# Attention and a SiLU feed-forward on one Trainium2 core: three products of the last eight token tiles done by seven quarter-size products each

## The chip, the cores and the metric

The kernel runs on one core of a Trainium2 chip. The metric is the time of one execution on the device, in microseconds (us). The engines are named as in the profile: PE (TensorE, matmuls), PEld (its weight loads), DVE (VectorE), ACT (ScalarE), POOL (GpSimd) and SP (SyncE, which here only issues stores).

## The reference

Eight batches of twelve heads of attention (448 tokens, head size 64), then a feed-forward with a SiLU gate over all 3584 tokens:

```python
scores = scale * np.matmul(q, k.transpose(0, 1, 3, 2))      # (8, 12, 448, 448)
attn = exp(scores - max) / sum
x = (attn @ v).transpose(0, 2, 1, 3).reshape(3584, 768)
h = x @ w_in                                                 # (3584, 2048)
g = h / (1.0 + np.exp(-h))
out = g @ w_out                                              # (3584, 768)
```

## The kernel before

One Python function plans the whole order of work. It holds a model of the engines' times and of the buffers that come free (`Op`, `Order`, `Ring`, `Banks`), goes through time event by event, lets each engine take the ready instruction with the lowest time plus bias, and at the end records all instructions in that order. So each engine's order is fixed when the program is built, and any new instruction can shift its neighbours.

**Stages.** Scores, exponentials and the product with V of the eight batches come first, with the first feed-forward layer (`ffn1`) of earlier batches between them. The last four batches do the first layer in two groups of two batches (`PAIRS`), with seven products in place of eight (`pair_product`; PE rows `f`, DVE adds of L881, ACT copies of L877 and gates of L889). The gated values lie in `G` as 128 partitions of the feed-forward dimension, 16 blocks `f`, by tokens; the seventh token tile of every second batch lies in `X`. `w_in_t` and `w_out_t` hold the weights.

**The second layer** is out = g @ w_out. Its unit is a "quad" `qd`: a pair of token tiles of 128 tokens, 14 pairs in all. Pair 0 is done by plain matmuls (`plain`). Pairs 1 to 13 each use the seven-product scheme on a 2 x 2 split: rows are the two tiles a and b, the inner dimension is cut into blocks 0 to 7 and 8 to 15, and the 768 output columns into two halves of `OH` = 384. `product(qd, m, ...)` (L678 by way of `times`) does product m: eight matmuls of 128 x 128 weights, which are gated values or sums of them, against 384 columns of `W_[m]`. `W_[1]`, `W_[2]`, `W_[3]` and `W_[7]` are parts of `w_out_t`, of which part 7 has been overwritten with a difference; `W_[4]`, `W_[5]` and `W_[6]` are sums in own tiles (names `D`). The sums of tile rows are made on DVE by `combine_g` (L911) into three tiles `S`; sum 7 overwrites `G`.

The products add up in banks of PSUM, and reads between them take the state out:

```python
BANK = {1: 1, 6: 1, 7: 1, 4: 1, 2: 2, 5: 5, 3: 5}
OUT = {1: (0, 0), 5: (1, 1), 6: (0, 1), 4: (1, 0)}   # ACT copies the bank (take_copy, L999)
SUM = {2: (0, 0), 7: (1, 1), 3: (0, 1)}              # DVE adds the bank (take_sum, L1013)
```

So bank 1 holds 1, then 1+6, then 1+6+7, then 1+6+7+4. The four parts (i, j) of the output, tile i and column half j, are gathered in SBUF tiles `ost` of 128 x 384 floats; when a part is complete `store` (L992) issues it, four issues of 32 rows on SP for most tiles, fewer and partly on ACT's queue for pairs 12 and 13. Pairs 11 and 13 (`FAR`) have their `ost` in old `xT` buffers, pair 8 (`WIDE`) in two old `E` buffers, and the others in a ring of four (`NOST`).

`queue_quad` (L1520) queues the products in the order 1, 5, 6, 2, 7, 3, 4; the last pair's order is 1, 5, 6, 7, 3, 4 and then 2 in two halves of 192 columns, whose reads and stores are `take_end` (L1005, L1009). The planner moves single matmuls among these to fill waits.

Of the kernel before, what the change touches and what calls it, by code (L numbers as in the profile page):

```python
# [9 lines left out]
FP16 = mybir.dt.float16  # L10
# [23 lines left out]
def act(n):  # L34
    return n * 0.00087 + 0.13
# [6 lines left out]
class Ring:  # L42
# [8 lines left out]
    def when(self, n):  # L51
        return heapq.nsmallest(n, self.free)[-1] if len(self.free) >= n else None
# [162 lines left out]
def kernel(  # L215
# [736 lines left out]
    def bank(qd, m):  # L952
        return pr_t[(qd, m)][:, 0:OH]
# [3 lines left out]
    def ost(qd, i, j):  # L957
        name = f"ost_{qd}_{i}{j}"
        if qd in FAR:
            t = sb.tile([128, 3, S], FP16, name=name, tag="xT", bufs=NX3)  # L960
            t = t.rearrange("p c t -> p (c t)")[:, 0 : 2 * OH].bitcast(FP32)
        elif qd == WIDE:
            at, x = int(i != j), j
            if at not in wide_t:
                wide_t[at] = sb.tile(
                    [128, HG, S], FP16, name=f"wide_{at}",
                    tag=f"E{e_slot[f'sx_{PAIRS[0]}_{at + 1}']}", bufs=1,
                )
            t = wide_t[at].rearrange("p h s -> p (h s)").bitcast(FP32)
            t = t[:, S * x : S * x + OH]  # L970
        else:
            t = sb.tile([128, OH], FP32, name=name, tag="ost", bufs=NOST)
        ost_t[(qd, i, j)] = t
        return t

    def store(qd, i, j):
        u, t = divmod(2 * qd + i, NT)
        w, turn = 0, 0
        while w < 4:
            r, col = divmod(128 * t + 32 * w, S)  # L980
            b = 2 * u + r
# [10 lines left out]
            eng.dma_start(out=dst, in_=ost_t[(qd, i, j)][32 * w : 32 * (w + n), :])  # L992
            w, turn = w + n, turn + 1
# [3 lines left out]

    def take_copy(qd, m):
        nc.scalar.copy(out=ost(qd, *OUT[m]), in_=bank(qd, BANK[m]))  # L999
        if m == 4:  # L1000
            store(qd, *OUT[m])

    def take_end(p, c0, c1):
# [3 lines left out]
        for lo, eng in ((0, nc.sync), (64, nc.scalar)) if c0 else ((0, nc.sync),):  # L1007
            hi = lo + 64 if c0 else 128
            eng.dma_start(out=out[row + lo : row + hi, c0:c1], in_=t[lo:hi])  # L1009

    def take_sum(qd, m):
        t = ost_t[(qd, *SUM[m])]
        nc.vector.tensor_tensor(out=t, in0=bank(qd, BANK[m]), in1=t, op=ALU.add)  # L1013
        store(qd, *SUM[m])


    units = []
    for b in range(B):
# [304 lines left out]

    def queue_pair_f(pb, f):
        done, lo = {}, f"w{f // 4 * 4}"
        before = chain[-1] if chain else None
        chain.append(done)

# [154 lines left out]
    def plan_sums():  # L1483

        if not quads:
            return
        qd, todo = quads[0]
        if len(todo) == 4:
            gates = {}
            for f in range(NFF):  # L1490
                gates[f] = gates_at(2 * qd, f) + gates_at(2 * qd + 1, f)
                if None in gates[f]:
                    return
            gates_of[qd] = gates
# [22 lines left out]
        if not todo:  # L1517
            quads.pop(0)

    def queue_quad(qd):  # L1520
        quads.append((qd, [5, 6, 7, 3]))
        took = {}
        home = far_ring if qd in FAR else wide_ring if qd == WIDE else ost_ring

        def read(m, deps):
            def then(at):
                if m in (2, 3, 4):
                    leave_bank(f"p_{qd}_{BANK[m]}")(at)
                if m in (2, 3, 4, 7):
                    home.give(at + STORE)  # L1530

            fn, eng = (take_copy, "ACT") if m in OUT else (take_sum, "DVE")
            busy = act(OH) if eng == "ACT" else OH / 960.0 + 0.13
            bias = -2 if eng == "ACT" else -4
            took[m] = od.add(Op(eng, busy, lambda: fn(qd, m), deps, bias, then=then))

        def queue(m, f0, f1, c0=0, c1=OH):
            first = {6: (1,), 2: (1,), 7: (6, 5), 3: (5, 6) if qd == LAST else (5, 6, 7), 4: (7,)}.get(m, ())

            def run():  # L1540
                strips = od.mode == "cols" and bool(qk_seq or av_seq)
# [22 lines left out]
                read(m, [op] + [took[x] for x in {2: (1,), 7: (5,), 3: (6,)}.get(m, ())])  # L1564

            def deps():
# [12 lines left out]
                return made + [x[0], (x[1], 4 * mm(OH))]  # L1579

            rings = ((home, 1),) if m in OUT and f0 == 0 else ()
            moe.append((deps, int(BANK[m] == m and f0 == 0), run, rings))


        begun = {}
        for m in (1, 5, 6, 2, 7, 3, 4) if qd < LAST else (1, 5, 6, 7, 3, 4):
            for f0 in range(0, HF, 1):
                queue(m, f0, f0 + 1)
        if qd == LAST:
# [350 lines left out]
    while True:  # L1940
# [2 lines left out]
        plan_pair()  # L1943
        plan_silu()
        plan_sums()
        soon = od.step()
        if od.free["PE"] <= od.now:
            ran = False
# [80 lines left out]
```

## Time and profile before

| | us |
|---|---|
| median of 3 runs (lowest to highest) | 379.64 (379.21 to 380.22) |
| the profiled execution, its own time | 379.18 |
| its span, first to last instruction | 377.4 |
| granted PE clock over the span | 0.998 |
| last stage, second layer of pairs 10 to 13: start to end | 338.4 to 373.9 |
| last matmul starts | 373.64 |
| last DVE read starts, and takes | 373.92, 0.36 |
| last store is issued (SP and ACT both) | 374.31 |

Rows of a group read: line, engine, operation, output<-input, shapes, count | busy us, mean ns of one | idle us of the engine just before them, and who ended it. Rows in order of time read: start us, length us, engine, line, operation, output<-input, shape, count, and in brackets the engine's idle time before. Rows that follow each other without a gap are merged, so two instructions that overlap in the pipe show a length below the sum of their own.

### The profile page before, as it was taken

The page shows a single profiled execution, that of the slowest core. Times are in us where ns is not written, and L with a number is a line of the kernel's source. Part 1 is how long each engine was busy: PE and PEld are TensorE (multiplying, and loading weights), DVE is VectorE, ACT ScalarE, POOL GpSimd, SP SyncE. Part 2 cuts the span into 40 slices and gives each one's busy share as a digit, 9 for nine tenths or more (in the row PEclk, how much of TensorE's full clock was granted, in tenths as well). Part 3 has the DMA queues.
Part 4 walks back from the last instruction along what each step waited for, and adds up shares of the span by engine and source line. Part 5 has one row for each costly group of instructions (what it writes and reads, how often), then busy time and mean ns, then how long its engine had stood idle before and what let it go on. Part 6 is the DMA issues. An engine that isn't in the chain of part 4 may idle for free.

```text
span 377.4 us, 9846 instructions
## 1 busy us (share of the span) xinstructions
PE 371.1 (98%) x3982; PEld 184.8 (49%) x3982; DVE 272.0 (72%) x556; ACT 255.5 (68%) x400; POOL 85.0 (23%) x155
## 2 busy tenths in 40 slices
PE   7999999999999999999999999999999999999996
PEld 3365445444444444444444444545556655556664
DVE  3668859989995969995969998898475424446441
ACT  4988873897878697868788777658872238882221
POOL 6652348333016326006423200000000000000000
PEclk9999999999999999999999999999999999999999
DMA  7999999918049849147955411200002330001332
GB/s 120 187 207 210 207 203 194 189 25 125 17 99 151 150 50 131 19 104 103 172 87 73 54 43 44 64 23 0 0 3 62 85 94 12 0 0 49 99 108 83
DMA packets 35982, 34.47 MB, mean 91 GB/s; under 512 B 11872, under 2 KB 35168, under 8 KB 35936
## 3 DMA queue, kind: packets, MB, share of 16 engines
q0 software_dynamic: 25312, 22.82, 40.8%
q1 hardware_dynamic: 10144, 10.48, 10.3%
q8 instruction: 31, 0.51, 0.5%
q10 hardware_dynamic: 480, 0.54, 0.4%
q14 instruction: 15, 0.12, 0.1%
HBM read 45.61 MB, written 11.01 MB: 150 GB/s over the span
## 4 chain that ended last, share of the span: by engine, by line
PE 95%; ACT 3%; DMA 1%; DVE 0%; issue 0%; POOLq 0%
PE p L678 32%; PE h L678 21%; PE f L678 16%; PE s L441 11%; PE a L563 8%; PE o L678 3%; ACT E L497 2%; PE a L549 2%; PE a L596 2%; DMA rk<-in_k_dram 1%; ACT T L486 1%; PE z L678 0%; PE p_2r L678 0%; DVE KT L390 0%; DVE ost L1005 0%
## 5 line engine op out<-in xcount | busy, mean ns | idle before, releaser
L497 ACT ACTIVATE E<-s 128x896 f16<-128x896 f32 x164 | 141.9, 921 | 24.5 <-PE s L441 24.5
L678 PE MATMUL h<-xT,w_in_t 128*32 128x448 f16 (+2 forms) x762 | 83.5, 348 | 0.0
L678 PEld LDWEIGHTS <-w_in_t 128*128 128x128 f16 (+1 forms) x909 | 54.6, 97 | 50.0 <-issue 8.1
L678 PEld LDWEIGHTS <-G 128*128 128x128 f16 (+1 forms) x684 | 44.0, 97 | 32.4 <-issue 5.0
L347 POOL DMA_DIRECT2D V<-in_v_dram x88 | 48.4, 561 | 50.1 <-PE a L563 29.2
L710 ACT ACTIVATE th<-h 128x448 f16<-128x448 f32 x67 | 36.6, 546 | 24.3 <-PE h L678 20.7
L678 PE MATMUL p<-w_out_t,G 128*128 128x384 f16 (+2 forms) x334 | 51.9, 324 | 0.0
L999 ACT COPY ost<-p 128x384 f32<-128x384 f32 x48 | 23.0, 479 | 42.1 <-PE p L678 32.4
L441 PE MATMUL s<-rq,KT 32*128 32x448 f16 (+3 forms) x728 | 44.8, 347 | 1.6 <-DVE rq L405 1.0
L678 PEld LDWEIGHTS <-S 128*128 128x128 f16 (+1 forms) x321 | 29.6, 98 | 23.1 <-issue 3.4
L1013 DVE TENSOR_TENSOR ost<-p,ost 128x384 f32<-128x384 f32 x35 | 19.4, 553 | 29.1 <-PE p L678 13.4
L754 DVE SCALAR_TENSOR_TENSOR G<-th,h 128x448 f16<-128x448 f16 (+1 forms) x64 | 35.7, 572 | 4.7 <-ACT th L710 4.3
L678 PE MATMUL p<-D,S 128*128 128x384 f16 (+1 forms) x217 | 37.5, 327 | 0.0
L563 PE MATMUL a<-E,V 128*32 128x448 f16 (+1 forms) x640 | 32.7, 356 | 0.0
L327 POOL DMA_DIRECT2D rq<-in_q_dram x25 | 14.0, 562 | 68.5 <-PE s L441 60.0
L666 DVE SCALAR_TENSOR_TENSOR xT<-a,rdn 128x448 f16<-128x448 f32 x46 | 26.9, 618 | 2.7 <-PE a L563 2.1
L441 PEld LDWEIGHTS <-KT 32*128 32x128 f16 (+1 forms) x824 | 12.3, 96 | 31.7 <-issue 29.5
L510 DVE TENSOR_TENSOR T<-T,E 128x1792 f16<-128x1792 f16 x21 | 22.8, 1085 | 4.9 <-ACT E L497 4.9
L510 DVE TENSOR_TENSOR T<-E,E 128x1792 f16<-128x1792 f16 x21 | 22.7, 1082 | 4.4 <-ACT E L497 4.4
L881 DVE TENSOR_TENSOR p<-f,p 128x448 f32<-128x448 f32 x15 | 9.3, 622 | 22.2 <-PE f L678 10.0
L678 PE MATMUL f<-sx,tw 128*128 128x448 f16 x102 | 23.4, 353 | 0.0
L563 PEld LDWEIGHTS <-V 128*32 128x32 f16 (+1 forms) x640 | 13.5, 95 | 18.1 <-issue 10.5
(101 smaller groups left out, 427.8 us busy)
## 6 DMA issues: line engine op xcount, KB each, us to landing
out_dram<-ost SPq DMA_DIRECT2D x179, 48.0 KB, 1.6
rk<-in_k_dram POOLq DMA_DIRECT2D x24, 224.0 KB, 5.3
rq<-in_q_dram POOLq DMA_DIRECT2D x23, 224.0 KB, 5.8
w_out_t<-in_moe_w_out_dram POOLq DMA_DIRECT2D x4, 768.0 KB, 13.0
V<-in_v_dram POOLq DMA_DIRECT2D x42, 64.0 KB, 4.3
V<-in_v_dram POOLq DMA_DIRECT2D x42, 48.0 KB, 4.5
w_in_t<-in_moe_w_in_dram POOLq DMA_DIRECT2D x6, 256.0 KB, 8.7
w_in_t<-in_moe_w_in_dram POOLq DMA_DIRECT2D x3, 512.0 KB, 12.4
```

Of the source, the lines that this page charges most:

```text
L327: nc.gpsimd.dma_start(out=rawq[n][:, cols], in_=group_of(q, b, hg)[:, cols])
L347: nc.gpsimd.dma_start(out=VT[b][32 * x : 32 * (x + 1), hs, at : at + count, :], in_=v[b, hs].rearrange("h (i g) d -> i h g d", g=TPP)[:, : ...
L441: nc.tensor.matmul(out=pS[p0 : p0 + 32 * (x1 - x0), h % 2, at : at + q1 - q0], lhsT=KT[(b, hg)][32 * h : 32 * (h + 1), key_rows(b, hg, c, ...
L497: nc.scalar.activation(out=E[(n, w)][:, 2 * y : 2 * y + 2, :], in_=pS_t[(n, w, y)][:, :, 0:S], func=AF.Exp, scale=attn_scale,)
L510: nc.vector.tensor_tensor(out=T[n], in0=T[n] if step else E[(n, 0)], in1=E[(n, step + 1)], op=ALU.add,)
L563: nc.tensor.matmul(out=a[32 * h : 32 * (h + 1), 0:S], lhsT=VT[b][k0:k1, HG * hg + h, place(b, hg, c), part - 1 :: 2], rhs=e[k0:k1, h], sta ...
L666: nc.vector.scalar_tensor_tensor(out=x3(b, cc)[:, cc % 3, 32 * g0 : 32 * g1], in0=acc[(n, part)][:, 0:nq], scalar=0.5, in1=rdn_t[n].rearra ...
L678: nc.tensor.matmul(out=out[i : i + cut], lhsT=w[:, i : i + cut], rhs=x, start=start, stop=stop, skip_group_check=True,)
L710: nc.scalar.activation(out=th, in_=h_t[(b, f, t0)][:, 0:n], func=AF.Tanh)
L754: nc.vector.scalar_tensor_tensor(out=dst[:, f, at + lo : at + hi], in0=th_t[(b, f, t0)][:, lo - t0 : hi - t0], scalar=1.0, in1=h_t[(b, f, ...
L999: nc.scalar.copy(out=ost(qd, *OUT[m]), in_=bank(qd, BANK[m]))
L1013: nc.vector.tensor_tensor(out=t, in0=bank(qd, BANK[m]), in1=t, op=ALU.add)
```

## The change

Product 2 of pair 10 and product 2 of pair 11 have the same right side, `W_[2]`; so have products 4 of 10 and 11, and products 4 of 12 and 13. Two such products together are again a 2 x 2 problem: rows are the two pairs' operands, the inner dimension is blocks 0 to 3 and 4 to 7, and the columns are two halves of 192. The change does each of these three joins (a "fold") by seven products of four matmuls of 192 columns, in place of two products of eight matmuls of 384.

```diff
-    WIDE = NT * B // 4 - 6
+    WIDE = (NT * B // 4 - 6, NT * B // 4 - 4)
+    FOLD = ((10, 11, (2, 4)), (12, 13, (4,)))
+    AHEAD_OF = ((1, 4),)
+    TAIL = None
...
+    def take_last(qd):
+        t = ost_t[(qd, *OUT[4])]
+        nc.vector.tensor_tensor(out=t, in0=bank(qd, 1), in1=t, op=ALU.add)
+        store(qd, *OUT[4])
...
+    def fold_w(m, i):
+        a, b = {
+            1: lambda: (right(m, 0, 1), right(m, 0, 0)),
+            2: lambda: (right(m, 1, 1), right_sum(m, 1)),
+            3: lambda: (right(m, 1, 1), right(m, 0, 1)),
+            4: lambda: (right(m, 1, 0), right_sum(m, 2)),
+        }[i]()
+        nc.vector.tensor_tensor(out=right_sum(m, i), in0=a, in1=b, op=ALU.subtract)
...
+        x, y, op = {
+            1: lambda: (left(b, m, 0), left(b, m, 1), ALU.add),
+            2: lambda: (x2_t[(g, m, 1)], left(a, m, 0), ALU.subtract),
+            3: lambda: (left(a, m, 0), left(b, m, 0), ALU.subtract),
+            4: lambda: (left(a, m, 1), x2_t[(g, m, 2)], ALU.subtract),
+        }[i]()
+        nc.vector.tensor_tensor(out=x2_t[(g, m, i)], in0=x, in1=y, op=op)
...
+        x, y, bank, at, new = {
+            1: lambda: (left(a, m, 0), right(m, 0, 0), "P", 0, True),
+            6: lambda: (x2_t[(g, m, 2)], right_sum(m, 2), "P", 0, False),
+            7: lambda: (x2_t[(g, m, 3)], right_sum(m, 3), "P", 0, False),
+            5: lambda: (x2_t[(g, m, 1)], right_sum(m, 1), "Q", 1, True),
+            4: lambda: (left(b, m, 1), right_sum(m, 4), "Q", 0, True),
+            2: lambda: (left(a, m, 1), right(m, 1, 0), "Q", 0, True),
+            3: lambda: (x2_t[(g, m, 4)], right(m, 1, 1), "Q", 1, False),
+        }[k]()
...
+        for f in range(4):
+            times(t, x[:, f, :], y[:, f, :], new and f == 0, f == 3, False)
...
+        if (g, m) in AHEAD_OF and k in (1, 6, 5):
+            at = slice(0, OH) if k == 5 else slice(OH // 2 * (k // 6), OH // 2 * (k // 6 + 1))
+            nc.scalar.copy(out=t[:, at], in_=bank[:, 0 : at.stop - at.start])
+            return
+        if k in (1, 6):
...
+            nc.vector.tensor_tensor(out=t[:, at], in0=bank[:, 0 : OH // 2], in1=t[:, at], op=ALU.add)
+        elif k == 7:
...
+                in0=bank[:, 0 : OH // 2].unsqueeze(1).to_broadcast([128, 2, OH // 2]),
...
+        else:
+            nc.vector.tensor_tensor(out=t, in0=bank[:, 0:OH], in1=t, op=ALU.add)
```

What each part does:

- `fold_w` makes four sums of weights for each of products 2 and 4, eight DVE instructions of 128 x 768. They are written over columns of `w_in_t` that the last first-layer products no longer read.
- `fold_x` makes four sums of tile rows for each fold, twelve DVE instructions of 128 x 512, the shape of `combine_g`, into old `KT`, `rk` and `rq` buffers.
- `fold_product` does the seven products of a fold in two banks, P and Q, of the PSUM buffers that the scores used. The queued order is 1, 4, 6, 5, 7, 3, 2. Product 6 waits for the read of product 1, product 7 for the read of 6, and product 3 for the read of 5, since they go on in the bank that is read.
- `fold_read` takes the banks out: k = 1 and 6 read 192 columns, k = 7 adds the same 192 columns to both halves, and k = 5 and 2 read 384. For pairs 10 and 11 all are DVE adds onto a part of the output that already holds the rest. For products 4 of 12 and 13 (`AHEAD_OF`), which come ahead of the rest of pair 12, reads 1, 6 and 5 are ACT copies into fresh tiles, and 7 and 2 DVE adds.
- Where product 4 is folded, bank 1 ends with 1+6+7. For pairs 10 and 11 ACT copies it after product 7, and the fold adds to that; for 12 and 13 `take_last` adds it on DVE after the read of product 7, and then stores the part (1, 0).
- `WIDE` now has pair 10 as well, whose output parts lie in the two old `E` buffers that pair 8 used.

In the built order PE has 84 matmuls of 192 columns more and 48 of 384 fewer, DVE has 32 instructions more, and ACT one copy more. PE's order is the same up to the last two first-layer blocks (f = 6 and 7), DVE's up to the first weight sum, which stands just ahead of them; from there on the matmuls of the folds stand among those of pairs 10 to 12. SP has the same number of issues, in another order.

More of the change, by code (lines that the diff above doesn't have):

```diff
@@ L999, in take_copy @@
         nc.scalar.copy(out=ost(qd, *OUT[m]), in_=bank(qd, BANK[m]))
-        if m == 4:
+        if m == 4 and (qd, m) not in folded:
             store(qd, *OUT[m])
@@ new lines, in fold_read @@
+    def fold_read(g, m, k):
+        a, b = FOLD[g][:2]
+        i, j = {2: SUM[2], 4: OUT[4]}[m]
+        bank = n2_t[(g, m, "P" if k in (1, 6, 7) else "Q")]
+        q = b if k in (7, 5) else a
+        if (g, m) in AHEAD_OF and k in (1, 5):
+            ost(q, i, j)
+        t = ost_t[(q, i, j)]
+        if (g, m) in AHEAD_OF and k in (1, 6, 5):
[3 more added lines that the diff above has]
+        if k in (1, 6):
+            at = slice(OH // 2 * (k // 6), OH // 2 * (k // 6 + 1))
+            nc.vector.tensor_tensor(out=t[:, at], in0=bank[:, 0 : OH // 2], in1=t[:, at], op=ALU.add)
+        elif k == 7:
+            v = t.rearrange("p (j n) -> p j n", j=2)
+            nc.vector.tensor_tensor(
+                out=v,
+                in0=bank[:, 0 : OH // 2].unsqueeze(1).to_broadcast([128, 2, OH // 2]),
+                in1=v,
+                op=ALU.add,
+            )
+            if (g, m) not in AHEAD_OF:
+                store(b, i, j)
+        else:
+            nc.vector.tensor_tensor(out=t, in0=bank[:, 0:OH], in1=t, op=ALU.add)
+            if k == 2 and (g, m) not in AHEAD_OF:
+                store(a, i, j)
@@ L1518, in plan_sums, with plan_folds @@
             quads.pop(0)
+    took_of, folds, x2_op, w2_op, pair_done = {}, [], {}, {}, {}
+    def plan_folds():
+        last = PAIRS[1]
+        if "w" not in w2_op and (last, 5) in pair_done:
+            made = [pair_done[(last, f)].get(m) for f in range(6) for m in range(1, 8)]
+            if None not in made:
+                w2_op["w"] = True
+                for m in sorted({m for *_, ms in FOLD for m in ms}):
+                    for i in (1, 2, 3, 4):
+                        more = [w2_op[(m, i // 2)]] if i in (2, 4) else []
+                        w2_op[(m, i)] = od.add(
+                            Op("DVE", 0.57, lambda m=m, i=i: fold_w(m, i), made + more, 1)
+                        )
+        if not folds or (last, HF - 1) not in pair_done:
+            return
+        g, m, done = folds[0]
+        made = [x for q in FOLD[g][:2] for f in range(HF, NFF) for x in gates_at(2 * q + m // 4, f)]
+        made += [pair_done[(last, HF - 1)].get((i, j)) for i in range(2) for j in range(2)]
+        n = len(x2_op) // 4
+        if n > 1:
+            made += [fold_done[n - 2].get(k) for k in (7, 2)]
+        if None in made:
+            return
+        folds.pop(0)
+        homes = [("KT", 3)] * 3 + [("rk", NRK)] if n % 2 else [("rq", NRQ)] * 4
+        for i in (1, 2, 3, 4):
+            more = [x2_op[(g, m, i // 2)]] if i in (2, 4) else []
+            x2_op[(g, m, i)] = od.add(
+                Op("DVE", 0.43, lambda i=i: fold_x(g, m, i, homes[i - 1]), made + more, 1)
+            )
@@ new lines, with queue_fold, read, queue @@
+    fold_done, ahead, ends = [], {}, []
+    def queue_fold(g, m):
+        a, b = FOLD[g][:2]
+        done, reads = {}, {}
+        fold_done.append(done)
+        folds.append((g, m, done))
+        first = {2: 1, 4: 4}[m]
+        early = (g, m) in AHEAD_OF
+        if early:
+            ahead[a] = lambda: when([reads.get(2)])
+            ahead[b] = lambda: when([reads.get(7)])
+        home = {q: far_ring if q in FAR else wide_ring if q in WIDE else ost_ring for q in (a, b)}
+        def read(k, busy, deps, then=None):
+            eng = "ACT" if early and k in (1, 6, 5) else "DVE"
+            busy = act(busy * 960.0 - 124.8) if eng == "ACT" else busy
+            reads[k] = od.add(Op(eng, busy, lambda: fold_read(g, m, k), deps, -4, then=then))
+        def queue(k):
+            rings = ((s_ring, 1),) if k in (1, 4) else ()
+            if early and k in (1, 5):
+                rings += ((home[a if k == 1 else b], 1),)
+            def run():
+                op = Op("PE", 4 * mm(OH // 2), lambda: fold_product(g, m, k), tail=PE_OUT)
+                for ring, need in rings:
+                    ring.take(need)
+                od.on_pe(op, "full", 4)
+                done[k] = op
+                narrow, wide = OH / 1920.0 + 0.13, OH / 960.0 + 0.13
+                if k == 1:
+                    read(1, narrow, [op] if early else [op, took_of[a][first]])
+                elif k == 6:
+                    read(6, narrow, [op, reads[1]])
+                elif k == 5:
+                    read(5, wide, [op, done[4]] if early else [op, done[4], took_of[b][first]])
+                elif k == 7:
+                    def then(at):
+                        s_ring.give(at)
+                        if not early:
+                            home[b].give(at + STORE)
+                    read(7, wide, [op, reads[5], reads[6]], then)
+                elif (g, m) == TAIL and k in (2, 3):
+                    at = OH // 2 * (k - 2)
+                    fn = lambda: take_end(n2_t[(g, m, "PQ"[k - 2])][:, at : at + OH // 2], at, at + OH // 2)
+                    od.add(Op("DVE", 0.33, fn, [op, reads[6]], -4))
+                elif k == 2:
+                    def then(at):
+                        s_ring.give(at)
+                        if not early:
+                            home[a].give(at + STORE)
+                    read(2, wide, [op, done[3], reads[5], reads[6]], then)
+            def deps():
+                made = [done.get(x) for x in {6: (1,), 5: (4,), 7: (6, 5), 3: (5,), 2: (3,)}.get(k, ())]
+                made += [reads.get(x) for x in {6: (1,), 7: (6,), 3: (5,)}.get(k, ())]
+                if not early:
+                    made += [took_of[a].get(first)] if k == 1 else [took_of[b].get(first)] if k == 4 else []
+                if (g, m) == TAIL and k in (2, 3):
+                    made = [pr_op.get((LAST, 3)), reads.get(7), reads.get(5)]
+                    made += [done.get(2)] if k == 3 else []
+                i = {5: 1, 6: 2, 7: 3, 3: 4}.get(k)
+                if i:
+                    made.append(x2_op.get((g, m, i)))
+                i = {5: 1, 6: 2, 7: 3, 4: 4}.get(k)
+                if i:
+                    made.append(w2_op.get((m, i)))
+                if not i:
+                    q = b if k == 4 else a
+                    made += [x for f in range(HF, NFF) for x in gates_at(2 * q + m // 4, f)]
+                return made
+            moe.append((deps, 0, run, rings))
+        for k in (1, 4, 6, 5, 7) if (g, m) == TAIL else (1, 4, 6, 5, 7, 3, 2):
+            queue(k)
+        if (g, m) == TAIL:
+            ends.append(lambda: [queue(k) for k in (2, 3)])
@@ L1564, in run, with then @@
                 read(m, [op] + [took[x] for x in {2: (1,), 7: (5,), 3: (6,)}.get(m, ())])
+                if m == 7 and (qd, 4) in folded:
+                    if qd in ahead:
+                        def then(at):
+                            leave_bank(f"p_{qd}_1")(at)
+                            home.give(at + STORE)
+                        od.add(
+                            Op(
+                                "DVE",
+                                OH / 960.0 + 0.13,
+                                lambda: take_last(qd),
+                                [op, took[7], ahead[qd]],
+                                -4,
+                                then=then,
+                            )
+                        )
+                    else:
+                        read(4, [op, took[7]])
             def deps():
@@ L1579, in deps @@
                 return made + [x[0], (x[1], 4 * mm(OH))]
-            rings = ((home, 1),) if m in OUT and f0 == 0 else ()
+            rings = ((home, 1),) if f0 == 0 and (m in OUT or m == 7 and (qd, 4) in folded and qd not in ahead) else ()
             moe.append((deps, int(BANK[m] == m and f0 == 0), run, rings))
         begun = {}
+        took_of[qd] = took
+        for g, k in AHEAD_OF:
+            if min(FOLD[g][:2]) - LEAD == qd:
+                queue_fold(g, k)
         for m in (1, 5, 6, 2, 7, 3, 4) if qd < LAST else (1, 5, 6, 7, 3, 4):
-            for f0 in range(0, HF, 1):
-                queue(m, f0, f0 + 1)
-        if qd == LAST:
+            if m == (3 if TAIL and qd == LAST else 4):
+                for g, (a, b, ms) in enumerate(FOLD):
+                    for k in ms if max(a, b) == qd else ():
+                        if (g, k) not in AHEAD_OF:
+                            queue_fold(g, k)
+            for f0 in range(0, HF, 1):
+                if (qd, m) not in folded:
+                    queue(m, f0, f0 + 1)
+        if qd == LAST and TAIL:
+            ends.pop()()
+        elif qd == LAST:
             for c in range(2):
```

44 lines of the change are left out of this document (37 added, 7 removed).

## Prediction

> **What bounds the kernel now.** I read the page first, then the busy time by stage, then the last 36 us in order of time, engine by engine.
>
> ```profile
> PE 371.1 (98%) x3982; PEld 184.8 (49%) x3982; DVE 272.0 (72%) x556; ACT 255.5 (68%) x400; POOL 85.0 (23%) x155
> ...
> PE   7999999999999999999999999999999999999996
> ...
> DVE  3668859989995969995969998898475424446441
> ```
>
> PE is full from the second slice to the last; DVE is at half or less in nine of the last ten slices, where the change works. The table by stretch (start:end, length, then busy time of PE, PEld, DVE, ACT, POOL) says the same of that stage:
>
> ```profile
> 338.40:373.90 35.50, 35.48 (x227) 21.70 (x224) 17.19 (x43) 8.08 (x17) 0.00 (x0) 1.00 0.29 77
> ```
>
> PE has 35.48 of 35.50 us and the full clock (1.00); DVE has 17.19. The question "is PE really paced by its matmuls" is answered by the timeline, whose merged rows give the pace:
>
> ```profile
> 347.70 2.76 PE L678 MATMUL p<-D,S 128*128 128x384 f16 x16
> ...
> 373.06 0.82 PE L678 MATMUL p_2r<-w_out_t,G 128*128 128x192 f16 x8
> ```
>
> A 384-column matmul alone is 0.326 us and 16 take 2.76, so one starts every (2.76 - 0.326)/15 = 0.162 us. The 192-column rows, which only the last pair of tiles has, are 0.246 alone and 8 take 0.82: one every (0.82 - 0.246)/7 = 0.082. So halving the columns halves the price, and a weight load per matmul (0.098 busy each) costs nothing at either width. PE never waits from 250 us to the last matmul; there is no stall to take away. What can be gained is PE work, and only that.
>
> **PE work.** Each of three folds takes away two products of 8 matmuls of 384 columns and adds seven of 4 matmuls of 192 columns: 16 x 0.1624 = 2.598 us against 28 x 0.0825 = 2.310 us (the paces above with one more digit, from single rows). That is 0.288 us each, 0.864 us for three. This is the whole prize: 0.23% of the time.
>
> **DVE work.** The rows that price it:
>
> ```profile
> L911 DVE TENSOR_TENSOR S<-G 128x512 f16<-128x512 f16 x8 | 3.1, 419 | 4.9 <-PE p L678 3.7 <-ACT G L889 1.1
> L1013 DVE TENSOR_TENSOR ost<-p,ost 128x384 f32<-128x384 f32 x11 | 6.1, 557 | 11.4 <-PE p L678 9.5 <-DMA out_dram<-ost 1.4 <-issue 0.4
> L1005 DVE TENSOR_TENSOR ost<-p,ost 128x192 f32<-128x192 f32 x1 | 0.4, 357 | 1.1 <-PE p L678 1.1
> ```
>
> - Eight weight sums of 768 elements: no row. Below 0.42 (512 elements, above), above 0.85 (1344, the sx rows); on the straight line 0.55. I take 0.55: 4.4 us. Seven stand among the last adds of L881, in a stretch (308.0 to 338.4) where DVE has 13.96 busy of 30.4 us, the eighth just behind them; they hide, but the add that the last f product of PE waits for comes late, by about 0.04 us.
> - Twelve sums of tile rows, the same shape as L911: 12 x 0.418 = 5.0 us.
> - Reads: four of 192 columns (0.357), eight of 384 and two `take_last` (0.557), less two L1013 that go: 4 x 0.357 + 8 x 0.557 = 5.9 us. Three of the 384 ones read 192 columns twice (a repeated operand); no row has that. Between 0.36 (if a repeated column were free) and 0.62 (the 448-column adds of L881) I take the 0.557 of equal output. ACT gets one copy more; it is 8.08 of 35.5 busy.
>
> So DVE goes from 17.2 to about 28 us in the last 35, and not evenly. In the changed order 47 instructions of DVE, from the second half of pair 10's first sum on, have next to no wait that isn't met already. I laid both lanes end to end. DVE's pace is below a duration, as these rows show: two sums in 0.75 mean 0.335 from start to start, and a read is followed after 0.47.
>
> ```profile
> 339.39 0.75 DVE L911 TENSOR_TENSOR S<-S,X 128x512 f16<-128x512 f16 x2
> ...
> 342.26 0.76 DVE L911 TENSOR_TENSOR S<-S,G 128x512 f16<-128x512 f16 x2
> 342.94 0.42 DVE L911 TENSOR_TENSOR G<-G 128x512 f16<-128x512 f16 x1
> 343.27 0.55 DVE L1013 TENSOR_TENSOR ost<-p,ost 128x384 f32<-128x384 f32 x1
> ...
> 346.52 0.56 DVE L1013 TENSOR_TENSOR ost<-p,ost 128x384 f32<-128x384 f32 x1 [1.42 <-DMA out_dram<-ost]
> ```
>
> DVE lane: the run starts at about 339.67 (ACT's last gate, later than before by the tile copy now ahead of it). Up to the read of product 1 in the fold of products 4 (pairs 10, 11) it has 30 x 0.335 + 6 x 0.474 + 0.275 = 13.17 us and one wait of 0.2 for PE: start 353.03, end 353.39. PE lane: the last f product starts at 337.71 + 2 x 0.162 + 0.04 = 338.07 (two tile matmuls now ahead of it) and is 3 x 0.189; then 32 matmuls of 192 and 75 of 384 come before product 6 of that fold, which waits for this read: 338.65 + 2.64 + 12.18 = 353.47. The read is there 0.08 us early. The other close ones: sum 5 and sum 6 of pair 10 (340.1 and 340.8) are 0.01 and 0.02 late; the bank that the next product opens (354.0) is free 0.10 early, the operand wanted at 356.1 is 0.14 early, two ACT copies for the third fold 0.1 early. All that waits behind each of these on PE is everything. With exact paces that sums to 0.07 us of new stalls.
>
> But DVE isn't that exact. The 342.26 row began 0.10 after its predecessor's end in place of 0.08 before it, because it waited for two semaphores, one of DVE's own; the 346.52 row began 0.4 later than anything it waited for. The run has eleven instructions with several semaphores, and beyond 0.08 us of slack each delay goes to PE in full. I take 0.25 us more: 0.3 us of stalls. Bounds: 0.07, and 1.9 (the first rival).
>
> [...]
>
> **The end.** The last issue of a store sets the end, 3.1 us after it:
>
> ```profile
> 371.56 1.39 ACTq L992 DMA_DIRECT2D out_dram<-ost  x2
> ...
> 373.60 0.39 ACTq L992 DMA_DIRECT2D out_dram<-ost  x1
> 373.68 1.09 SPq L1009 DMA_DIRECT2D out_dram<-ost  x2
> ...
> 374.31 0.50 ACTq L1009 DMA_DIRECT2D out_dram<-ost  x1
> ```
>
> Before, product 4 stands between 7 and the last half of 2, so the stores are spread. After, product 7's last matmul is only 4 x 0.162 + 14 x 0.082 = 1.80 us ahead of the very last one, and DVE reads three tiles of 0.47 and two of 0.27 in that time. Measured from the last matmul: third read ends at +0.14, its store can be issued at +0.2, and behind it on SP stand two issues of 0.47 and 0.35, on ACT one of 0.55 to 0.74, before the last: at +0.85 to +1.2. Before it was 374.31 - 373.64 = +0.67. I take 0.3 us lost at the end; bounds 0 (the fourth read hides, issues at their shortest) and 0.5. Stores of pairs 10 and 11 keep SP busy to about 363.5 in place of 359.7; nothing waits for them, as their tiles are no longer taken again by pairs 12 and 13.
>
> **Sum.** -0.86 + 0.30 + 0.30 = -0.26 us on the profiled execution's own 379.18 (span 377.4 and 1.8 around it). That execution lies 0.46 under the median 379.64, inside the spread of 379.21 to 380.22. Against the median: 379.4.
>
> **Rivals.**
>
> 1. DVE becomes the bound, and the kernel is slower. Place: the DVE run from 339.7 to 356.8 us. If each of the eleven instructions that wait for several semaphores loses the 0.18 us that the 342.26 row lost, that is 2.0 us, all but 0.08 of it on PE: -0.86 + 1.9 + 0.3 = +1.35, 381.0. It decides from 0.6 us of DVE delay on for any loss at all, and from 1.7 for one that can be measured. For: the 342.26 and 346.52 rows, and a slack of 0.1. Against: 8 sums in a row at 0.335, and most of these waits are for work long done. 0.18.
> 2. The full gain: no stall beyond 0.07, the end as now: -0.8, 378.8. For: PE's lane is never more than 0.04 short on paper. Against: the store issues at the end. 0.20.
> 3. The narrow matmuls are paced by their weight loads: 84 x (0.098 - 0.0825) = 1.3 us more, so +1.0, 380.7. Against: thirteen 192-column matmuls in the last 2 us at 0.082. 0.04. [...]
>
> That the change doesn't do what it says is excluded: the new order has 48 matmuls of 384 fewer and 84 of 192 more.
>
> **Chances and range.** Forecast (378.9 to 380.3) 0.55, rival 2 0.20, rival 1 0.18, rival 3 0.04, else 0.03. The range 378.5 to 380.9 takes the first two, rival 3 and the mild part of rival 1. About 0.3% (1.1 us) is what a measurement of this kernel can tell from no change. Faster by more would need more than the whole prize: 0.05. Slower by more is most of rival 1 and some of rival 3: 0.19. Within: 0.76.
>
> **What would show it.** PE work: no 192-column matmul slower than 0.083 from start to start. DVE: idle of under 0.5 us between 340 and 356, PE idle of 0.1 to 0.5 released by DVE, above all near 341 and 353. The end: last store issue 0.85 to 1.2 us after the last matmul. Wrong if PE idles over 0.6 us there, or if the new sums or repeated reads take longer than their rows.

## The result and the profile after

| | before | after |
|---|---|---|
| median, us (lowest to highest) | 379.45 (379.11 to 380.71), 22 runs | 380.45 (379.88 to 382.18), 22 runs |
| ratio, 95% interval | | 1.0023, 1.0013 to 1.0033 |
| profiled execution, its span | 379.18, 377.4 | 379.91, 378.1 |

The changed kernel is 0.2% **slower**: +0.9 us by the ratio, where I forecast -0.26. TensorE does get through its work earlier; the time is lost behind the last matmul. The page of the changed kernel:

```profile
PE 371.4 (98%) x4018; PEld 187.4 (50%) x4018; DVE 284.0 (75%) x588; ACT 255.7 (68%) x401; POOL 85.0 (22%) x155
...
PE   8999999999999999999999999999999999999994
...
DVE  3667959999995969995969998897575334489852
```

PE is as full as before and DVE works 12 us more (284.0 for 272.0), in the slices that were half empty. PE's last slice reads 4 where it read 6: each slice is 9.5 us, so a smaller share of the last one is matmul. That is the first sign that the end of the span, and not the stage, has grown. The table by stretch for the last stage:

```profile
338.40:373.10 34.70, 34.59 (x262) 23.93 (x260) 25.82 (x70) 8.49 (x19) 0.00 (x0) 1.00 0.26 70
```

PE is still full (34.59 of 34.70), at the full clock (1.00), and DVE has gone from 17.19 to 25.82. The rows in order of time, first where DVE was to be short, then at the end:

```profile
338.02 0.73 PE L683 MATMUL f<-xT,tw 128*128 128x448 f16 x3
...
339.56 2.76 PE L683 MATMUL p<-D,S 128*128 128x384 f16 x16
...
353.01 0.35 DVE L1101 TENSOR_TENSOR wide<-n_P,wide 128x192 f32<-128x192 f32 x1
...
353.41 0.49 PE L683 MATMUL n_P<-w_in_t,fold 128*128 128x192 f16 x4
...
371.97 1.39 SPq L997 DMA_DIRECT2D out_dram<-ost  x2
371.97 2.14 ACTq L997 DMA_DIRECT2D out_dram<-ost  x3
372.17 0.82 PE L683 MATMUL p_2r<-w_out_t,G 128*128 128x192 f16 x8
...
373.05 0.34 DVE L1010 TENSOR_TENSOR ost<-p_2r,ost 128x192 f32<-128x192 f32 x1
373.46 1.17 SPq L1014 DMA_DIRECT2D out_dram<-ost  x2
374.23 0.54 ACTq L1014 DMA_DIRECT2D out_dram<-ost  x1
```

The close read at 353 us starts where the lane had it (353.01 for 353.03) and PE goes on without a gap; paces are 2.76 for 16 and 0.82 for 8, as before. At the end the last DVE read is over at 373.39, but ACT issues the last store at 374.23, because ACT's queue is busy with the three issues of the row before it (1.95 of the 2.14 us from 371.97). Before, that issue came 0.03 us behind DVE. Then the transfers themselves. The view of DMA from 371 to 378 us, 40 slices of 0.175 us each (first line: how busy the 16 DMA engines are, in tenths; second: what they moved), and its list of issues (count, size of each, median us from issue to landing, which is when the store is reported done). Before:

```profile
DMA  0000000002998989972089998477300000000000
GB/s 0 0 0 0 0 0 0 0 0 70 211 211 246 351 264 255 299 255 88 9 325 355 373 334 264 119 185 198 88 0 0 0 0 0 0 0 0 0 0 0
...
out_dram<-ost ACTq DMA_DIRECT2D x1, 192.0 KB, 2.1
...
out_dram<-ost ACTq DMA_DIRECT2D x1, 48.0 KB, 2.1
```

After:

```profile
DMA  0000000000009789549798799999873100000000
GB/s 0 0 0 0 0 0 0 0 0 0 0 0 228 158 193 369 176 123 176 114 167 228 263 307 290 312 373 343 281 224 123 31 18 0 0 0 0 0 0 0
...
out_dram<-ost ACTq DMA_DIRECT2D x1, 192.0 KB, 3.7
...
out_dram<-ost ACTq DMA_DIRECT2D x1, 48.0 KB, 2.9
```

Both move the same 768 KB of the last pair of tiles. Before, they start at 372.6 and there is a hole in the middle; after, they start at 373.1, without a hole, and in most of the first nine slices the engines are 0.7 to 0.9 busy while they move 114 to 228 GB/s; in the tenth to sixteenth they move 228 to 373 with the same share of busy time. The last store lands 2.93 us after its issue in place of 2.11.

The reason for the late start: in the changed kernel two outputs of the last pair, (1, 1) and (1, 0), are complete only with its product 7. Before, product 4 and the rest of product 2 stood behind it, and its read began at 370.97, 2.67 us ahead of the last matmul. After, product 4 is folded and stands ahead of product 7; the read begins at 371.38, 1.37 us ahead of a last matmul that is 0.89 us earlier (372.75 for 373.64). So the first store comes 0.41 us **later**, although PE ends earlier, and the reads that complete all four outputs run in the 2.0 us from 371.38 to 373.39.

**Theory A**: the end is set by issue and drain of the last pair's four stores, which can't begin before product 7; the third fold crowds them. Rivals: DVE takes the gain back; the order has nothing to do with it, and the end is longer for another reason ("chance" in the expectations).

### The profile page after: what moved, and what is told of

The parts are those of the page before. It is cut to its first block, busy times and chain, and to the rows that moved or that the text cites. A ratio compares the mean times of both kernels' runs of the same rounds, so it can differ in the third digit from the quotient of the medians.

```text
span 378.1 us, 9953 instructions
## 1 busy us (share of the span) xinstructions
PE 371.4 (98%) x4018; PEld 187.4 (50%) x4018; DVE 284.0 (75%) x588; ACT 255.7 (68%) x401; POOL 85.0 (22%) x155
## 4 chain that ended last, share of the span: by engine, by line
PE 96%; DMA 1%; ACT 1%; DVE 1%; issue 0%; DVEq 0%; POOLq 0%
PE p L683 29%; PE h L683 21%; PE f L683 16%; PE s L446 12%; PE a L568 8%; PE o L683 3%; PE a L554 2%; PE a L601 2%; PE n_Q L683 1%; DMA rk<-in_k_dram 1%; PE n_P L683 1%; ACT T L491 1%; PE z L2180 0%; PE z L683 0%; DVE ost L1023 0%
## 5 line engine op out<-in xcount | busy, mean ns | idle before, releaser
L683 PEld LDWEIGHTS <-G 128*128 128x128 f16 (+1 forms) x672 | 42.5, 97 | 29.7 <-issue 5.0
L683 PE MATMUL p<-w_out_t,G 128*128 128x384 f16 (+2 forms) x326 | 50.9, 324 | 0.0
L1004 ACT COPY ost<-p 128x384 f32<-128x384 f32 x42 | 20.1, 480 | 31.8 <-PE p L683 20.6
L683 PE MATMUL p<-D,S 128*128 128x384 f16 (+1 forms) x217 | 38.8, 326 | 0.0
L1023 DVE TENSOR_TENSOR ost<-p,ost 128x384 f32<-128x384 f32 x31 | 17.1, 552 | 23.7 <-ACT ost L1004 12.6
```

The lines of the kernel that those rows point to most:

```text
L683: nc.tensor.matmul(out=out[i : i + cut], lhsT=w[:, i : i + cut], rhs=x, start=start, stop=stop, skip_group_check=True,)
```

## The experiments

Each kernel is compared with the kernel before on the same chip.

**1. Two folds, without the third.**

```diff
-    FOLD = ((10, 11, (2, 4)), (12, 13, (4,)))
-    AHEAD_OF = ((1, 4),)
+    FOLD = ((10, 11, (2, 4)),)
+    AHEAD_OF = ()
```

> Only the two folds of pairs 10 and 11 are kept; pairs 12 and 13 work as in the kernel before. Theory A (the third fold puts the last pair's product 4 ahead of its product 7, so that all four stores of the last pair become ready in the last 1.8 us and the end is set by their issue and drain): the last matmul is 0.58 us earlier than before (2 x 0.288) and everything behind it is as before (last issue about 0.67 us after the last matmul's start, landing 2.1 us later): -0.58 us, 378.9 us. Rival DVE (VectorE full from 339.6 to 356.7 takes back what TensorE saves): it has two thirds of the added reads and sums in the same stretch, so the gain is gone here too: -0.1 to +0.3 us. Rival chance (the end after the change is as it is for a reason that has nothing to do with the order): +0.5 to +1.

379.08 for 379.56, ratio 0.9985 (0.9976 to 0.9995): -0.6 us. The last issue is 0.68 us behind the last matmul and lands 2.12 later, as before. The folds of pairs 10 and 11 give what their matmuls save; DVE takes nothing back.

**2. The third fold alone.**

```diff
-    FOLD = ((10, 11, (2, 4)), (12, 13, (4,)))
-    AHEAD_OF = ((1, 4),)
+    FOLD = ((12, 13, (4,)),)
+    AHEAD_OF = ((0, 4),)
```

> Only the third fold (product 4 of pairs 12 and 13) is kept; pairs 10 and 11 work as in the kernel before. Theory A: -0.29 us on TensorE and +1.6 us behind the last matmul, as in the changed kernel: +1.3 us, 380.8 us, slower than the whole change. Rival DVE: a third of the added VectorE work, so about a third of the loss: +0.3 us. Rival chance: -0.3 to 0.

380.92, ratio 1.0029 (1.0017 to 1.0041): +1.1 us, with less DVE work than the first run. The end is that of the changed kernel:

```profile
372.68 1.39 SPq L997 DMA_DIRECT2D out_dram<-ost  x2
372.69 2.14 ACTq L997 DMA_DIRECT2D out_dram<-ost  x3
...
374.94 0.53 ACTq L1014 DMA_DIRECT2D out_dram<-ost  x1
```

ACT issues for 2.14 us with gaps of 0.1 us or less, and comes to the last store 1.48 us behind the last matmul (373.47). Runs 1 and 2 together put the whole loss on the third fold; the rival DVE is out.

**3. The third fold on product 2.** The same saving, another place: product 4 of the last pair stays behind product 7, and the last two small products of the fold end the kernel. The switches were in the changed kernel already.

```diff
-    FOLD = ((10, 11, (2, 4)), (12, 13, (4,)))
-    AHEAD_OF = ((1, 4),)
-    TAIL = None
+    FOLD = ((10, 11, (2, 4)), (13, 12, (2,)))
+    AHEAD_OF = ()
+    TAIL = (1, 2)
```

> The third fold takes product 2 of pairs 12 and 13 in place of product 4, and its last two small products end the kernel; product 4 of the last pair stays behind product 7. The same work as the change on TensorE, but 4.1 us of it (20 narrow and 15 wide matmuls) lie behind product 7, in place of 1.8 us; one store of pair 12 comes into the end as well (960 KB in place of 768). Theory A: the last matmul is 0.86 us earlier than before, last issue 0.7 to 1.0 us after it, last landing 2.1 to 2.5 us after that: -0.5 to -0.86 us, 378.7 us. Rival DVE: as the change, +0.9 us. Rival chance: +0.5 to +1.

378.70, ratio 0.9981 (0.9969 to 0.9992): -0.7 us. Three folds are a gain over the kernel before where the stores are spread. Over the two folds of run 1 the third adds only 0.05 us by the traces (0.31 saved on PE, 0.25 lost again at the end; table below), too little for the timing to show. The rival chance is out as well.

**4. Whole stores.** Two outputs of the last pair are stored in halves of 64 rows on both queues; here each goes in one transfer of 128 rows, and the store of the first half of the last output moves from SP's queue to ACT's. The last half of the last output still goes in two transfers of 64 rows.

```diff
-                n = 4 if w == 0 and (qd < LAST or (i, j) == OUT[4]) else 2
+                n = 4 if w == 0 else 2
...
-        for lo, eng in ((0, nc.sync), (64, nc.scalar)) if c0 else ((0, nc.sync),):
+        for lo, eng in ((0, nc.sync), (64, nc.scalar)) if c0 else ((0, nc.scalar),):
```

> The changed kernel; each output of the last pair but the last half is stored by one transfer in place of two halves on two queues (6 issues in place of 8, the first half of the last output by ScalarE's queue). Theory A has two halves that this tells apart. If the 16 DMA engines' drain of 768 KB sets the end, the last landing stays where it is, 377.1 us, though the last issue comes 0.5 to 0.8 us earlier: within 0.2 us of the changed kernel, +0.7 to +1.1 us against before. If the issuing instructions on ScalarE and SyncE (0.47 to 0.76 us each) set it, the time falls with the last issue: +0.1 to +0.4 us against before.

378.88, ratio 0.9986 (0.9974 to 0.9998): -0.5 us, 1.4 us better than the changed kernel and better than either half of the theory allowed. The order of the matmuls is that of the changed kernel; only the end is another:

```profile
372.43 1.26 SPq L997 DMA_DIRECT2D out_dram<-ost  x2
...
372.90 0.36 ACTq L997 DMA_DIRECT2D out_dram<-ost  x1
...
373.68 0.99 ACTq L1014 DMA_DIRECT2D out_dram<-ost  x2
373.93 0.47 SPq L1014 DMA_DIRECT2D out_dram<-ost  x1
```

```profile
DMA  0000000000000899999999899940000000000000
GB/s 0 0 0 0 0 0 0 0 0 0 0 0 0 316 386 334 395 342 369 387 351 386 290 316 233 273 119 0 0 0 0 0 0 0 0 0 0 0 0 0
```

The same 768 KB now leave at 316 to 395 GB/s in the first nine slices and are through in 2.4 us in place of 3.6. The 128-row issues take 0.33 to 0.36 us, where ACT's 128-row issue took 0.76 in the changed kernel. I had set issue and drain against each other; the form of the stores sets both.

**5. Whole stores in the kernel before**, the same edit of the stores on it.

> The kernel before, nothing folded, with the stores of the fourth run: each output of the last pair but the last half in one transfer of 128 rows. Theory crowd (the 64-row halves cost the end only where the change crowds them): before, the last issue already came 0.03 us behind VectorE's last read, so there is little to win, 0 to -0.15 us. Rival form (halves of 64 rows are slow to issue and to drain wherever they are, and the gain of the fourth run has little to do with the change): -0.4 us or more.

379.54 for 379.60, ratio 0.9999 (0.9990 to 1.0008). Nothing in sum, as the crowd theory says, but two effects cancel in the trace: the landing is 0.17 us shorter, and the last issue 0.24 later, since ACT is still issuing the store that the edit moved to it. Run 12, without that delay, shows by its trace that the halves cost some 0.3 us here too, against 1.6 where the outputs come together.

**6. Halves by columns.** Eight issues on the same queues as in the changed kernel.

```diff
+            if qd == LAST and (i, j) != OUT[4]:
+                for c, eng in ((0, nc.sync), (OH // 2, nc.scalar)):
+                    eng.dma_start(out=dst[:, c : c + OH // 2], in_=tile_[:, c : c + OH // 2])
```

> The changed kernel with its eight issues at the end, but the two outputs of the last pair that are stored by two queues are halved by columns (128 rows of 192) in place of rows (64 rows of 384). Same bytes, same number of issues on the same queues. If the number of issues on a queue is what delays the end: +0.7 to +0.9 us against before, as the changed kernel. If the form of 64 rows is what costs (0.47 to 0.55 us to issue against 0.34 to 0.36 for 128 rows, and 100 to 235 ns for a packet against 64 to 70 ns): -0.3 to -0.7 us.

378.98, ratio 0.9981 (0.9972 to 0.9990): -0.7 us. It isn't the number of issues. The same bytes and the same number of issues, with the two outputs in halves of 128 rows in place of 64, are 1.6 us faster by the timing and 1.3 by the traces:

```profile
GB/s 0 0 0 0 0 0 0 0 0 0 0 0 0 0 4 272 320 316 360 316 395 334 312 329 307 316 307 193 198 215 0 0 0 0 0 0 0 0 0 0
...
out_dram<-ost ACTq DMA_DIRECT2D x1, 192.0 KB, 2.0
```

**7. Fewer bytes, the same issues.**

```diff
+            m = 128 if qd == LAST and (i, j) == OUT[4] else OH
-            eng.dma_start(out=dst, in_=ost_t[(qd, i, j)][32 * w : 32 * (w + n), :])
+            eng.dma_start(out=dst[:, 0:m], in_=ost_t[(qd, i, j)][32 * w : 32 * (w + n), 0:m])
```

> The changed kernel, but only 128 of the 384 columns of the output that product 4 of the last pair completes are stored (128 KB fewer bytes; the rest of that output is left unwritten); the issues and their order are the same. If the drain of the bytes sets the end: 128 KB at about 200 KB per us are 0.64 us, so +0.1 to +0.4 us against before. If the issues and the 64-row form set it: as the changed kernel, +0.7 to +0.9 us.

379.92, ratio 1.0007 (0.9998 to 1.0016): +0.3 us, in the range of the drain, with an interval that overlaps that of the changed kernel by a little. The trace parts it: the last issue is still 1.48 us behind the last matmul, to the hundredth, but it lands 2.38 us later in place of 2.93. So of the 1.6 us that the end has lost about half is issuing (+0.81), which fewer bytes don't change; the other half is the longer landing (+0.82), and 128 KB fewer take 0.55 off that.

**8. Run 3 with the whole stores of run 4.**

> The third run (the third fold takes product 2 of pairs 12 and 13, not product 4) with the whole stores of the fourth. In the third run SyncE issued the last store 0.15 us after it could have; with whole stores that wait goes and the landing is 2.0 us in place of 2.0 to 2.3: -0.15 to -0.3 us against the third run, -1.0 to -1.2 us against before, the best of the versions so far. If the whole stores help only where product 4 is ahead of product 7: -0.86 us, as the third run.

378.82, ratio 0.9979 (0.9970 to 0.9989): -0.8 us, the same as run 3 and less than the -1.0 to -1.2 expected. My edit gave the first half of the last output to ACT, which was still issuing another store; so ACT came to the last store 1.15 us behind the last matmul, later than in run 3 (0.82).

**9. The queues of the halves exchanged.**

```diff
-            eng = nc.scalar if turn % 2 and 4 * qd + 8 >= NT * B else nc.sync
+            eng = nc.scalar if (turn + (qd == LAST)) % 2 and 4 * qd + 8 >= NT * B else nc.sync
```

> The changed kernel with the two queues of the last pair's row halves exchanged: rows 0 to 63 by ScalarE's queue, rows 64 to 127 by SyncE's. In the changed kernel SyncE's halves drained at 100 to 235 ns a packet and ScalarE's at 66 to 70. If that follows the rows (partitions 0 to 63), ScalarE's queue is the slow one now; if it follows the queue or the order of issue, SyncE's stays slow. The time: as the changed kernel in both cases, +0.6 to +0.9 us against before.

380.00 for 379.63, ratio 1.0009 (0.9998 to 1.0020): +0.3 us (+0.6 by the trace), less than expected, its interval overlapping that of the changed kernel. The edit exchanges the queues of the two outputs whose stores `store` issues, not those of the last half of the last output. The slow packets stay on SP's queue (91 to 187 ns by quarters of a microsecond up to 375.5 us, ACT's 65 to 83), now with the other rows. They don't follow the rows. Whether they follow the queue or the order is not separated: SP's half is the first to drain here as well (from 373.64, ACT's from 374.09; in the changed kernel 373.10 and 373.55).

**10. Run 4 with the last half in one transfer too**, by SP: no 64-row transfer is left in the last pair.

> The fourth run (the change with whole stores) with its last half output in one transfer of 128 rows of 192 by SyncE, in place of two of 64 rows: no transfer of 64 rows is left in the last pair. In the fourth run ScalarE issued the last one 0.2 us after SyncE's, since it was still issuing the half before. If the 64-row form costs here too: 0.25 us less than the fourth run, -0.8 to -1.0 us against before. If it doesn't: -0.6 us, as the fourth run.

378.65, ratio 0.9974 (0.9964 to 0.9984): **-1.0 us**, better than both kernels.

```profile
372.69 1.26 SPq L997 DMA_DIRECT2D out_dram<-ost  x2
...
373.16 0.36 ACTq L997 DMA_DIRECT2D out_dram<-ost  x1
...
373.94 0.36 ACTq L1013 DMA_DIRECT2D out_dram<-ost  x1
374.19 0.33 SPq L1013 DMA_DIRECT2D out_dram<-ost  x1
```

The last issue waits for nothing but DVE's last read, 0.71 us behind the last matmul (373.48).

**11. Run 3 with no 64-row store of the last pair**, and neither queue behind.

> The third run (fold of product 2) with no 64-row store of the last pair: whole stores, the first half of the last output by SyncE and the second by ScalarE, each in one transfer. In the run before this one with whole stores ScalarE issued the last store 0.47 us late, behind the half that I had given it; here neither waits. Expected 0.3 us less than that run and than the third: -1.0 to -1.2 us against before. If the tail has a floor that stores of this kind can't lower: -0.8 us.

378.66, ratio 0.9983 (0.9972 to 0.9994): -0.6 us, with an interval 0.8 us wide. Less than expected; by its trace (below) it should be as good as run 10, and the timing can't part the two.

**12. The kernel before with these stores.**

> The kernel before, nothing folded, with the same stores as the run above: no transfer of 64 rows in the last pair. It says what the store form alone is worth where the stores are spread: 0 to -0.2 us. What the folds are worth with the end set right is then the difference of the two runs above to this one: -0.7 to -0.9 us if all that TensorE saves reaches the end.

379.21, ratio 0.9990 (0.9981 to 1.0000): -0.4 us, a little more than expected. So the three folds with the end set right are worth 0.6 us (0.9990 to 0.9974, run 10) by the timing, each of the two ratios being good to 0.4 us, and 0.5 (run 10) to 0.7 (run 11) by the traces; I expected 0.7 to 0.9. Of the 0.8 that PE saves, up to 0.3 is lost again at the end.

All runs by their traces. The second column is from the hundredth-last matmul of the first layer (318.4 us before), ahead of all that the change touches, to the last matmul; then last issue behind last matmul, last landing behind last issue; the sum of the three against that of before; and the measured ratio as us of 379.6.

| kernel | to the last matmul | to the last issue | to its landing | sum against before | measured |
|---|---|---|---|---|---|
| before | 55.25 | 0.67 | 2.11 | | |
| after | 54.45 | 1.48 | 2.93 | +0.8 | +0.9 |
| 1 two folds | 54.74 | 0.68 | 2.12 | -0.5 | -0.6 |
| 2 third fold | 55.03 | 1.48 | 2.84 | +1.3 | +1.1 |
| 3 fold of product 2 | 54.43 | 0.82 | 2.23 | -0.6 | -0.7 |
| 4 whole stores | 54.45 | 0.91 | 1.98 | -0.7 | -0.5 |
| 5 before, whole | 55.25 | 0.91 | 1.94 | +0.1 | -0.0 |
| 6 column halves | 54.45 | 1.07 | 2.02 | -0.5 | -0.7 |
| 7 fewer bytes | 54.45 | 1.48 | 2.38 | +0.3 | +0.3 |
| 8 = 3 with whole | 54.43 | 1.15 | 1.91 | -0.6 | -0.8 |
| 9 queues exchanged | 54.45 | 1.48 | 2.68 | +0.6 | +0.3 |
| 10 no 64-row store | 54.45 | 0.71 | 2.07 | -0.8 | -1.0 |
| 11 = 3, no 64-row store | 54.43 | 0.67 | 1.96 | -1.0 | -0.6 |
| 12 before, no 64-row store | 55.25 | 0.67 | 1.84 | -0.3 | -0.4 |

The three durations, from one trace of each kernel, give the size of every run's change within 0.4 us, and the sign of all but run 5, where both figures are within 0.1 us of nothing. Run 10 has the changed kernel's order of matmuls, and its end takes 0.71 + 2.07 = 2.78 us, as long as before (0.67 + 2.11). So crowding the outputs costs nothing by itself: the loss of 1.6 us at the end needs the crowd and the row halves together.

## Why the prediction was wrong, step by step

- **PE work, -0.864: right.** The stretch to the last matmul is 55.25 us with no fold, 55.03 with one (run 2), 54.74 with two (run 1), 54.45 with three: 0.22 for the first, which also brings the new gap of the next item, and 0.29 for each further fold, where I had 0.288. No 192-column matmul started later than 0.083 behind the one before it; rival 3 is out.
- **New stalls, +0.30: too much.** PE has one new gap, 0.065 us at 338.02, in the wait for the last first-layer add, which I had at 0.04. There is none above 0.004 in the DVE run. Its lane was right to 0.02 us at the read at 353, and the margin of 0.25 that I put on it for several-semaphore waits was not needed. The rows for which I had no measurement were right too: the weight sums took 0.548 (I had 0.55), the reads with a repeated operand 0.550 (0.557). -0.864 + 0.065 = -0.80; the column shows -0.80. Rival 1 (DVE becomes the bound) is out: DVE is full from 339.6 to 356.8 (16.87 busy of 17.20 us) and PE misses nothing.
- **The end, +0.30 with bounds 0 and 0.5: this step failed.** It is 5.38 us from the start of the last matmul to the end of the span (378.13), where it was 3.76: +1.62. The sentence that failed first is "The last issue of a store sets the end, 3.1 us after it". I carried that 3.1 over; it came out at 3.90, since the 768 KB drained with a backlog (+0.8). The second is the issue, put at +0.85 to +1.2 and measured at +1.48 (+0.8 against +0.67). I had seen that the three outputs come together and had counted the queues behind them, but with issue times from rows where the two queues hardly met: ACT's four took 0.54, 0.76, 0.65 and 0.54, where I had "on ACT one of 0.55 to 0.74" ahead of the last. The second of them, of 128 rows, ran until 373.36, so the third began 0.71 us after the last matmul and not at +0.2.
- **Sum**: -0.864 + 0.065 + 1.62 = +0.82. The measured ratio says +0.87. The profiled spans differ by 0.7, since the last stage began 0.08 earlier in that execution.
- **Rival 2** (full gain, 0.20) had PE right and named what spoke against it, the store issues at the end. What I lacked was a rival in which the end loses more than PE gains. My slower rival was on DVE, the engine that had the most new work; the engine that lost was the queue with the same work in less time.

Why 64 rows cost more is told in part by the runs.

(a) **Issuing**: a 64-row issue took 0.47 us even with the other queue idle (run 11, SP at 371.55), a 128-row one 0.34 to 0.36 (run 4, SP at 372.43, ACT at 372.90). Near 64-row issues the others got longer. In the changed kernel ACT's 128-row issue took 0.76 us, against 0.36 in run 4 with SP idle; narrow windows of the timeline show the single rows that are merged above:

```profile
372.60 0.76 ACTq L997 DMA_DIRECT2D out_dram<-ost  x1
...
372.89 0.47 SPq L997 DMA_DIRECT2D out_dram<-ost  x1
```

An issue that runs on the other queue at the same time would explain that only in part: the issue that got longer is the one that began first, the other took its usual 0.47, and two issues of 128 rows that began together (run 6, both at 372.78) took 0.34 and 0.38. The issue just before on the same queue may matter as well. In run 11 SP's 128-row issue, 0.09 us behind its 64-row one, took 0.54 us with ACT idle:

```profile
372.12 0.54 SPq L997 DMA_DIRECT2D out_dram<-ost  x1
```

ACT's 0.76 also came 0.1 us behind a 64-row issue of its own. Which of the two stretches it stays open.

(b) **Draining**: the first half to go moved at 158 to 228 GB/s with the engines 0.7 to 0.9 busy (the first three slices after 373.1 above), the 128-row stores of run 4 at 316 to 395. Its partner on ACT's queue wasn't slow: packets of 65 to 70 ns and a slice at 369 GB/s of which it moved 302 (after) and 343 (run 9), with rows 64 to 127 (after) and with rows 0 to 63 (run 9). Why SP's half is the slow one stays open. It isn't the crowd alone: the first half was as slow before the change (102 to 121 ns a packet, 95 to 120 in the changed kernel), where the drain had time to end before the last stores came.

## What to carry to other kernels

When work is moved ahead of the step that completes the last outputs, lay out the end as carefully as the engine that is saved: count when each output is complete, how long each queue is solid with issues, and whether the bytes can drain in the time that is left; a landing time read where stores are spread doesn't hold where they meet (2.11 us before, 2.93 after). Here two folds in work that no store needed as cover gave what their matmuls save (0.6 us); the third, which took away work that stood behind the last pair's product 7, lost 1.1 us where it should have gained 0.3. Where stores crowd the end, send each as one transfer of all 128 partitions; if it must be halved, halve it by columns and not by rows. Columns alone turned +0.9 us into -0.7 here (run 6), whole transfers into -1.0 (run 10).

## What the runs showed of the hardware that I had not expected

- A store of 64 rows took longer to issue than one of 128 rows: 0.47 us against 0.34 to 0.36, each with the other queue idle (runs 11 and 4).
- Around 64-row issues a 128-row issue got longer: 0.76 us against 0.36 on ACT, 0.54 on SP in run 11 with ACT idle. Two 128-row issues that met hardly did (0.34 and 0.38, run 6).
- Row halves on SP's queue drained at 91 to 235 ns a packet of 1536 bytes (means of quarters of a microsecond, after and run 9), the 128-row stores of runs 4 and 10 at 62 to 70.
- The hundredth-last first-layer matmul, ahead of all the edits, starts between 318.18 and 319.16 us in the fourteen traces. A difference of two spans below 1 us says little by itself; durations counted from a common instruction are steadier: the stretch to the last matmul is the same within 0.01 us in the six traces with the changed kernel's order (54.45) and in the three with the order before (55.25).
